# A decode attention block with a long cache: softmax and PV moved into the loop round of their own head, loads K K V V, one score buffer

## The chip, the cores and the metric

One core of one Trainium2 chip. The metric is the device time of one execution in microseconds (us). The kernel before takes 422.17 us, the median of three runs (422.05 to 422.44). Verdicts call a difference of under 2% "same".

## The reference, cut to what matters

```python
# B=2 tokens (one per batch), 32 query heads, 4 KV heads, cache of 32768 keys, head size 128
mod = (silu(c) @ w_mod)                               # 6 shifts, scales and gates
h = layernorm(x) * (1 + ca) + sa
q = h @ wq
for each of the 8 pairs (batch b, KV head g):         # 8 query heads share one KV head
    scores = q[8 heads] @ K[b, g].T * 128 ** -0.5     # K: 32768 x 128, 8.4 MB in bf16
    p = softmax(scores)
    o = p @ V[b, g]                                   # V: 8.4 MB
x = x + ga * (o @ wo)
x = x + gb * (gelu(layernorm(layernorm(x)*(1+cb)+sb) @ w1 + b1) @ w2 + b2)
```

The caches are 134 MB of the 178 MB that have to be read. From here on a "head" is one of the eight pairs (b, g).

## The kernel before

K lies in memory with keys as rows, and the score matmul needs it turned. So for each head TensorE (PE) transposes 256 tiles of 128 keys, eight to a PSUM bank; VectorE (DVE) and ScalarE (ACT) copy the banks to SBUF; and PE multiplies each turned tile with the eight queries. ACT copies the scores to SBUF, DVE takes the maxima, ACT does eight exps (one for each query head), and PE multiplies with V.

The kernel is written as a software pipeline. PE and DVE run a hardware loop with one round per head. Round i transposes K of head i and computes its scores; the "lagged" parts do softmax and PV of head i-1 in between. The last head's softmax and PV stand after the loop. All loads go in one list, in order, through the queue of SyncE (SP). K and V move in halves of 4 MB; the ring has one slot for each: first K half, second K half, first V half, second V half.

```python
def tr(i, cc, g8):   # eight transposes into psKT[g8 % 4], then one eviction by DVE or ACT
    ...
def qk(i, cc, g8):   # eight score matmuls; after each chunk cc: ACT copies scores, DVE takes the max
    ...
        Sc = S_sb[i % 2][:, :, cc * TPC:(cc + 1) * TPC]      # two score buffers
    ...
# order of loads
add_kv("K", 0, 0); add_kv("K", 0, 1)
order = [("K", 0), ("V", 0), ("K", 1), ("V", 1)]
early = [("V", 0), ("K", 0), ("K", 1), ("V", 1)]
for i in range(1, NBG + 1):
    for kind, hf in early if i == 1 else order:
        if kind == "V":  add_kv("V", i - 1, hf)
        elif i < NBG:    add_kv("K", i, hf)
# the loop, one round per head
for i in range(NBG):
    lagged(softmax_1)                            # lagged: of head i - 1, skipped in the first round
    for cc in range(NCH):                        # 4 chunks of 8 groups of 8 tiles
        for g8 in range(TPC // 8):
            tr(i, cc, g8)
            pipe.append((i, cc, g8))
            if len(pipe) > PIPE: qk(*pipe.pop(0))
            if (cc, g8) == (0, 1):   lagged(softmax_2)
            elif (cc, g8) == (0, 4): lagged(softmax_3)
            elif i and (0, 4) < (cc, g8) and exps: exp(i - 1, exps.pop(0))
        if cc == 1:   lagged(lambda: pv(i - 1, 0), row_sums, lambda: pv(i - 1, 1))
        elif cc == 3: lagged(lambda: pv(i - 1, 2), lambda: pv(i - 1, 3))
    lagged(extract)
    while pipe: qk(*pipe.pop(0))
    lagged(lambda: extract_2(i - 1))
...
# after the loop: softmax, PV and extraction of the last head, then wo, w1, w2
```

## Time and profile before

| what | value |
|---|---|
| time, median | 422.17 us |
| share of the 16 DMA engines' span in use by the load queue | 98.9% |
| bytes | 178.3 MB, 434 GB/s between first load (3.9 us) and last landing (414.5 us) |
| PE waiting for K | 45.1 us |
| period of a head | 38.7 us |

The page of the profile follows in lines. The first line is PE's busy time. The next four are 40 equal slices of the span: PE's busy tenths, the granted PE clock in tenths, the DMA engines' busy tenths, and GB/s. Then come the load queue, the shares of the chain that ended last, and two groups of instructions (the transposes of K and the PV matmuls) with busy time, mean ns of one, and idle time before them.

```profile
...
PE 296.6 (71%) x5171; PEld 237.6 (57%) x5171; DVE 166.9 (40%) x347; ACT 156.2 (37%) x269; POOL 6.0 (1%) x31
...
PE   1547429869988767695969686976859693645566
...
PEclk9999999988999997988888896989887888655575
DMA  8999999999999999999999999999999999999995
GB/s 335 430 430 420 437 440 443 411 437 446 409 443 443 424 430 443 433 421 443 440 418 443 437 418 440 443 415 440 449 412 440 446 416 437 423 429 423 428 426 244
...
q1 hardware_dynamic: 9714, 178.28, 98.9%
...
DMA 70%; PE 26%; ACT 2%; SPq 1%; issue 0%; DVE 0%
...
L543 PE MATMUL psKT<-ident,K 128*128 128x128 bf16 x2048 | 174.0, 237 | 46.1 <-DMA K<-in_A_k_cache_dram 45.1
...
L586 PE MATMUL psO<-V,E_sb 128*32 128x512 bf16 x512 | 33.9, 401 | 1.3 <-ACT E_sb L576 1.3
...
```

DMA is at nine tenths in every slice between the first and the last. That is the sign of a kernel bound by its loads: no engine's work can shorten it, as long as no wait holds the loads up. The Trainium skill ("DMA: Bandwidth & Descriptors", Bandwidth, Where 436 GB/s comes from) gives 435 GB/s as the ceiling of the ports into SBUF; this trace shows 434.

The view of waits (who waited for whom, us in total, times, longest) says how PE stands to the loads:

```profile
...
PE psKT L543 <- DMA K<-in_A_k_cache_dram: 45.1, 13, 6.4
...
```

PE waits 13 times for K, which is slack of PE. Here is PE in one round, from the timeline (start, us, engine, line, operation, output<-inputs, count, and in brackets the idle time before it and what ended it):

```profile
...
295.45 0.62 PE L543 MATMUL psKT<-ident,K 128*128 128x128 bf16 x8 [3.72 <-DMA K<-in_A_k_cache_dram]
...
307.18 1.91 PE L586 MATMUL psO<-V,E_sb 128*32 128x512 bf16 x32
309.02 0.76 PE L555 MATMUL psS<-qcur,KT_sb 128*128 128x8 bf16 x24
310.79 0.48 PE L606 MATMUL psM<-msum,hmat 128*128 128x128 f32 x2 [1.01 <-DVE msum L601]
314.75 1.89 PE L543 MATMUL psKT<-ident,K 128*128 128x128 bf16 x16 [3.48 <-DMA K<-in_A_k_cache_dram]
...
```

PE starts the second half of K when it lands (295.45), does PV of the head before at 307.18 in the middle of the stream, and then waits 3.48 us for the next head's K. After the loop the last head's softmax and PV ran alone, with nothing under them:

```profile
...
348.94 0.75 PE L555 MATMUL psS<-qcur,KT_sb 128*128 128x8 bf16 x24
...
349.73 0.60 ACT L559 ACTIVATE S_sb<-psS 128x512 f32<-128x512 f32 x1 [2.33 <-PE psS L555]
...
353.93 0.51 ACT L576 ACTIVATE E_sb<-S_sb,negm 128x256 bf16<-128x256 f32 x1 [3.60 <-DVE negm L572]
...
358.99 0.23 DVE L593 COPY rsum<-rowsum 128x128 f32<-128x128 f32 x1 [5.16 <-ACT E_sb L576]
...
359.79 5.83 PE L586 MATMUL psO<-V,E_sb 128*32 128x512 bf16 x64
...
```

From the end of the last scores (349.7) to the first exp 4.2 us (0.8 of which is another head's work on DVE), eight exps to 359.0, and 64 PV matmuls in 5.83 us. The other PV groups of before take 1.05 to 1.9 us for 16 to 32 matmuls.

### The profile page before, as it was taken

How to read it: one execution, taken by the hardware profiler on the slowest of the kernel's cores; microseconds unless marked ns; L12 is line 12 of the kernel's file. 1: busy time of each engine (PE TensorE's matmuls, PEld its weight loads, DVE VectorE, ACT ScalarE, POOL GpSimd, SP SyncE). 2: the span in 40 equal slices, each digit the busy share in tenths (PEclk: the TensorE clock that was granted, in tenths of full speed). 3: DMA queues.
4: the chain of work that ended last, by engine and by line, in shares of the span. 5: the costliest groups of instructions: out<-in, count | busy, mean ns of one | idle time of the engine just before them, and what ended most of it. 6: DMA issues, size and time to landing. Idle time of an engine off the chain costs nothing.

```text
span 420.3 us, 11591 instructions
## 1 busy us (share of the span) xinstructions
PE 296.6 (71%) x5171; PEld 237.6 (57%) x5171; DVE 166.9 (40%) x347; ACT 156.2 (37%) x269; POOL 6.0 (1%) x31
## 2 busy tenths in 40 slices
PE   1547429869988767695969686976859693645566
PEld 1105109859878657494949575764849492212244
DVE  1102005645676454354536452653555363101311
ACT  2000005538548334551636282446426364200020
POOL 3000000000000000000000000000000000000000
PEclk9999999988999997988888896989887888655575
DMA  8999999999999999999999999999999999999995
GB/s 335 430 430 420 437 440 443 411 437 446 409 443 443 424 430 443 433 421 443 440 418 443 437 418 440 443 415 440 449 412 440 446 416 437 423 429 423 428 426 244
DMA packets 9727, 178.46 MB, mean 425 GB/s; under 512 B 1002, under 2 KB 1009, under 8 KB 2291
## 3 DMA queue, kind: packets, MB, share of 16 engines
q1 hardware_dynamic: 9714, 178.28, 98.9%
q8 instruction: 9, 0.15, 0.1%
q14 instruction: 4, 0.02, 0.0%
HBM read 178.28 MB, written 0.00 MB: 424 GB/s over the span
## 4 chain that ended last, share of the span: by engine, by line
DMA 70%; PE 26%; ACT 2%; SPq 1%; issue 0%; DVE 0%
DMA K<-in_A_k_cache_dram 51%; PE psKT L543 18%; DMA wo<-in_A_wo_dram 8%; DMA w<-in_B_w_dram 7%; PE psS L555 5%; DMA wmod<-in_w_mod_dram 4%; ACT E_sb L576 1%; PE psO L586 1%; SPq L415 1%; ACT KT_sb L547 1%; PE psO L759 1%; PE psS L680 0%; ACT L576 0%; PE psM L566 0%; ACT S_sb L559 0%
## 5 line engine op out<-in xcount | busy, mean ns | idle before, releaser
L543 PE MATMUL psKT<-ident,K 128*128 128x128 bf16 x2048 | 174.0, 237 | 46.1 <-DMA K<-in_A_k_cache_dram 45.1
L543 PEld LDWEIGHTS psKT<-ident,K 128*128 128x128 bf16 x2048 | 133.7, 106 | 53.7 <-DMA K<-in_A_k_cache_dram 49.2
L549 DVE COPY KT_sb<-psKT 128x1024 bf16<-128x1024 bf16 x160 | 107.8, 689 | 107.0 <-PE psKT L543 107.0
L547 ACT ACTIVATE KT_sb<-psKT 128x1024 bf16<-128x1024 bf16 x96 | 98.0, 1021 | 128.4 <-PE psKT L543 128.4
L555 PE MATMUL psS<-qcur,KT_sb 128*128 128x8 bf16 x2048 | 88.1, 167 | 7.7 <-ACT KT_sb L547 6.4
L555 PEld LDWEIGHTS psS<-qcur,KT_sb 128*128 128x128 bf16 x2048 | 79.0, 98 | 12.7 <-ACT KT_sb L547 7.6
L576 ACT ACTIVATE E_sb<-S_sb,negm 128x256 bf16<-128x256 f32 x64 | 32.3, 504 | 8.1 <-DVE negm L572 7.1
L586 PE MATMUL psO<-V,E_sb 128*32 128x512 bf16 x512 | 33.9, 401 | 1.3 <-ACT E_sb L576 1.3
L560 DVE TENSOR_REDUCE m1c<-psS 128x8 f32<-128x512 f32 x32 | 22.1, 690 | 14.8 <-ACT S_sb L559 14.1
L559 ACT ACTIVATE S_sb<-psS 128x512 f32<-128x512 f32 x32 | 18.9, 592 | 18.9 <-PE psS L555 18.9
L586 PEld LDWEIGHTS psO<-V,E_sb 128*32 128x32 bf16 x512 | 12.2, 100 | 13.1 <-issue 4.2
L491 PE MATMUL psS<-wmod,inT 128*32 128x512 bf16 x64 | 8.4, 622 | 11.9 <-DMA wmod<-in_w_mod_dram 11.9
L680 PE MATMUL psS<-wo,atT 128*32 128x512 bf16 x64 | 7.6, 627 | 10.8 <-DMA wo<-in_A_wo_dram 10.8
L462 ACT ACTIVATE stat<-stat 128x2 f32<-128x2 f32 x3 | 0.6, 203 | 35.4 <-DVE stat L461 35.4
L512 PE MATMUL psS<-wq,inT 128*32 128x512 bf16 x64 | 7.6, 627 | 7.1 <-DMA wq<-in_A_wq_dram 6.1
L576 ACT ACTIVATION_READ_ACCUMULATOR E_sb<-S_sb,negm 128x1 f32 x64 | 12.1, 189 | 0.0
L491 PEld LDWEIGHTS psS<-wmod,inT 128*32 128x32 bf16 x64 | 1.3, 112 | 17.9 <-DMA wmod<-in_w_mod_dram 17.4
L680 PEld LDWEIGHTS psS<-wo,atT 128*32 128x32 bf16 x64 | 1.9, 128 | 15.4 <-DMA wo<-in_A_wo_dram 9.4
L606 PE MATMUL psM<-msum,hmat 128*128 128x128 f32 x16 | 4.2, 346 | 7.1 <-DVE msum L601 7.1
L497 ACT ACTIVATE S_sb<-psS 128x512 f32<-128x512 f32 x1 | 0.6, 597 | 22.8 <-DVE S_sb L499 22.8
L499 DVE COPY S_sb<-psS 128x512 f32<-128x512 f32 x1 | 0.7, 692 | 20.6 <-PE psS L491 20.6
L599 DVE TENSOR_SCALAR msum<-psO,mk 128x128 f32<-128x128 f32 x8 | 2.8, 351 | 15.0 <-PE psO L586 15.0
(116 smaller groups left out, 136.4 us busy)
## 6 DMA issues: line engine op xcount, KB each, us to landing
K<-in_A_k_cache_dram SPq DMA_DIRECT2D x16, 4096.0 KB, 25.6
V<-in_A_v_cache_dram SPq DMA_DIRECT2D x16, 4096.0 KB, 32.5
wmod<-in_w_mod_dram SPq DMA_DIRECT2D x8, 1536.0 KB, 16.4
wq<-in_A_wq_dram SPq DMA_DIRECT2D x4, 2048.0 KB, 37.7
wo<-in_A_wo_dram SPq DMA_DIRECT2D x4, 2048.0 KB, 25.3
w<-in_B_w_dram SPq DMA_DIRECT2D x4, 1792.0 KB, 35.8
w<-in_B_w_dram SPq DMA_DIRECT2D x3, 2048.0 KB, 30.4
w<-in_B_w_dram SPq DMA_DIRECT2D x1, 768.0 KB, 27.9
```

Source lines behind the costliest of these rows:

```text
L415: T.dma("sp", lambda e, dst=dst, src=cur.src: e.dma_start(dst, src), key=cur.sem, writes=[cur.reg], frees=old)
L491: pe(lambda e, w=it.view, k=k, ch=ch, n=n, q=q: e.matmul(bank[n][32 * q:32 * q + 32, :], lhsT=inT[:, k, :], rhs=w[:, ch * 512:(ch + 1) * 512],
L512: pe(lambda e, w=it.view, k=k, ch=ch, n=n, q=q: e.matmul(bank[n][32 * q:32 * q + 32, :], lhsT=inT[:, k, :], rhs=w[:, k % 2, ch * 512:(ch + ...
L543: pe(lambda e, kq=kq, jj=jj, w=kt, t=t: e.transpose(psKT[kq][:, jj * 128:(jj + 1) * 128], w[:, t, :], ident[:, :]), reads=[it.reg, "ident" ...
L547: act(lambda e, src=src: e.activation(KT_sb[g8][:, :, :], src, ACT.Copy), reads=[f"psKT{kq}"], writes=[f"KT_sb{g8}"], sem=f"ev{cc}_{g8}")
L549: dve(lambda e, src=src: e.tensor_copy(KT_sb[g8][:, :, :], src), reads=[f"psKT{kq}"], writes=[f"KT_sb{g8}"], sem=f"ev{cc}_{g8}")
L555: pe(lambda e, t=t, jj=jj: e.matmul(ps[:, t * HPG:(t + 1) * HPG], lhsT=KT_sb[g8][:, jj, :], rhs=qcur[:, :], start=True, stop=True), reads= ...
L559: act(lambda e: e.activation(Sc, ps[:, :].rearrange("p (t h) -> p h t", h=HPG), ACT.Copy), reads=[preg], writes=[f"S_sb{i % 2}_{cc}"], sem ...
L560: dve(lambda e: e.tensor_reduce(m1c[:, :, cc], ps[:, :].rearrange("p (t h) -> p h t", h=HPG), AX.X, ALU.max), reads=[preg], writes=[f"m1c{ ...
L576: act(lambda e: e.activation(E_sb[:, :, h, :], S_sb[j][:, h, :].rearrange("p (u t) -> p u t", t=4), ACT.Exp, bias=negm[:, h:h + 1], scale= ...
L586: pe(lambda e, t4=t4, tg=tg, q=q: e.matmul(psO[32 * q:32 * q + 32, :], lhsT=E_sb[:, tg // 4, :, :].rearrange("p h t -> p (h t)"), rhs=vt[: ...
L680: pe(lambda e, w=it.view, g=g, j=j, hf=hf, q=q: e.matmul(psS[0][32 * q:32 * q + 32, :], lhsT=atT[g][:, j, :], rhs=w[:, j, hf * 512:(hf + 1 ...
```

## The change

The intent is a simpler loop: each head is finished in its own round, first K, then V, with no "lagged" parts, no branches in the loop, one score buffer in place of two, and no attention code after the loop. The price is that PE stands still while the softmax of a head runs. The work itself (bytes, matmuls, copies, exps) is unchanged.

```diff
-    S_sb = [sb(f"S_sb{i}", [128, HPG, NT]) for i in range(2)]
+    S_sb = sb("S_sb", [128, HPG, NT])
...
-    add_kv("K", 0, 0)
-    add_kv("K", 0, 1)
-    order = [("K", 0), ("V", 0), ("K", 1), ("V", 1)]
-    early = [("V", 0), ("K", 0), ("K", 1), ("V", 1)]
-    for i in range(1, NBG + 1):
-        for kind, hf in early if i == 1 else order:
-            if kind == "V":
-                add_kv("V", i - 1, hf)
-            elif i < NBG:
-                add_kv("K", i, hf)
+    for i in range(NBG):
+        for kind in "KV":
+            for hf in range(2):
+                add_kv(kind, i, hf)
...
     for i in range(NBG):
-        lagged(softmax_1)
         for cc in range(NCH):
             for g8 in range(TPC // 8):
                 tr(i, cc, g8)
...
-                if (cc, g8) == (0, 1):
-                    lagged(softmax_2)
-                elif (cc, g8) == (0, 4):
-                    lagged(softmax_3)
-                elif i and (0, 4) < (cc, g8) and exps:
-                    exp(i - 1, exps.pop(0))
-            if cc == 1:
-                lagged(lambda: pv(i - 1, 0), row_sums, lambda: pv(i - 1, 1))
-            elif cc == 3:
-                lagged(lambda: pv(i - 1, 2), lambda: pv(i - 1, 3))
-        lagged(extract)
         while pipe:
             qk(*pipe.pop(0))
-        lagged(lambda: extract_2(i - 1))
+        softmax_1()
+        softmax_2()
+        softmax_3()
+        for h in range(HPG):
+            exp(h)
+        row_sums()
+        for cc in range(NCH):
+            pv(i, cc)
+        extract()
+        extract_2(i)
...   (cut: the helper that folds the rounds into a loop loses its lagged parts; the copy of
       softmax, PV and extraction after the loop goes; ring offsets of the K and V halves and of w1 move)
```

More of the change, by code (lines that the diff above doesn't have):

```diff
@@ L34 @@
 RING = 160 * 1024
+AHEAD = ("sc2", "sc3", "pk", "ac")
 EVAC_PATTERN = ("dve", "act", "dve", "act", "dve", "dve", "act", "dve")
@@ L41 @@
     LOOPED = ("pe", "dve")
-    PE_KEYS = ("pe", "pl")
     def __init__(self, nc):
@@ L55, in __init__ @@
         self.segments = None
-        self.lag = False
     def key(self, name, given=0, step=None):
@@ L116, in _dep_tokens @@
         if E == "pe":
-            tokens = [t for t in tokens if t[0] not in self.PE_KEYS]
+            tokens = [t for t in tokens if t[0] != "pe"]
         return tokens
@@ L130, in _put @@
         if self.segments is not None and E in self.LOOPED:
-            self.segments[E][-1][1].append(op)
+            self.segments[E].append(op)
         else:
@@ L168, in raw @@
         self._put(E, ("raw", [], fn, None))
-    def part(self, lag):
-        self.lag = lag
-        for E in self.LOOPED:
-            self.segments[E].append((lag, []))
     def fold(self, rounds):
@@ L180, in _fold @@
         first = min(rounds)
-        full = rounds[max(rounds)]
         body = []
-        for n, (lag, ops) in enumerate(full):
-            merged = []
-            for k, (kind, _, fn, extra) in enumerate(ops):
-                offs = {}
-                for it, segs in rounds.items():
-                    same, other = segs[n]
-                    assert same == lag
-                    if not other and lag and it == first:
-                        continue
-                    assert len(other) == len(ops) and other[k][0] == kind and other[k][3] == extra
-                    for key, val in other[k][1]:
-                        off = val - self.step[key] * it
-                        assert offs.setdefault(key, off) == off, (E, n, k, key, it, val, offs)
-                waits = []
-                for key, off in offs.items():
-                    assert self.step[key] * (first + lag) + off > 0, (E, n, k, key, off)
-                    waits.append((key, self.step[key], off))
-                merged.append((kind, waits, fn, extra))
-            if merged:
-                body.append((lag, merged))
+        for k, (kind, _, fn, extra) in enumerate(rounds[max(rounds)]):
+            offs = {}
+            for it, ops in rounds.items():
+                assert len(ops) == len(rounds[first]) and ops[k][0] == kind and ops[k][3] == extra
+                for key, val in ops[k][1]:
+                    off = val - self.step[key] * it
+                    assert offs.setdefault(key, off) == off, (E, k, key, it, val, offs)
+            for key, off in offs.items():
+                assert self.step[key] * first + off > 0, (E, k, key, off)
+            body.append((kind, [(key, self.step[key], off) for key, off in offs.items()], fn, extra))
         self.ops[E].append(("loop", [], body, (first, max(rounds) + 1)))
@@ L218, in _loop @@
     def _loop(self, eng, E, body, bounds):
-        pairs = [w[1:] for _, ops in body for op in ops for w in op[1]]
+        pairs = [w[1:] for op in body for w in op[1]]
         often = [p for p in dict.fromkeys(pairs) if p != (1, 0) and pairs.count(p) > 1]
@@ L227, in wait @@
                 eng.wait_ge(self.sem[w[0]], val[w[1:]] if w[1:] in val else it * w[1] + w[2])
-            for lag, ops in body:
-                def run():
-                    for op in ops:
-                        self._emit(eng, E, op, wait)
-                if lag:
-                    with eng.If(it > bounds[0]):
-                        run()
-                else:
-                    run()
+            for op in body:
+                self._emit(eng, E, op, wait)
     def emit(self, block):
@@ L272, in bass_adaLN_cond__gqa_block_cached__mixer_channel_mlp__decode_kernel @@
     T = Tracker(nc)
-    for name, step, given in (("pe", 64, 0), ("pl", 8, 8), ("dve", 4, 0), ("dl", 4, 4)):
-        T.key(name, given)
-        T.step[name] = step
+    T.step["pe"], T.step["dve"] = 72, 8
     def sb(name, shape, dtype=FP32):
@@ L331, in bass_adaLN_cond__gqa_block_cached__mixer_channel_mlp__decode_kernel @@
     rinv = sb("rinv", [128, 1])
-    S_sb = [sb(f"S_sb{i}", [128, HPG, NT]) for i in range(2)]
-    row = S_sb[0].rearrange("p h n -> p (h n)")
-    ROW = [f"S_sb0_{cc}" for cc in range(NCH)]
+    S_sb = sb("S_sb", [128, HPG, NT])
+    row = S_sb.rearrange("p h n -> p (h n)")
+    ROW = [f"S_sb_{cc}" for cc in range(NCH)]
     E_sb = sb("E_sb", [128, NT // 4, HPG, 4], BF16)
@@ L368, in add @@
         by_key[key] = it
-    SLOT = {("K", 0): 0, ("V", 0): 1, ("K", 1): 2, ("V", 1): 3}
     def add_kv(kind, i, hf):
@@ L376, in add_kv @@
         add((kind, i, hf), [2, TPC * D], cache[b, g][r0:r0 + 2 * CH_ROWS, :].rearrange("(p c t) d -> p c (t d)", c=2, p=128),
-            SLOT[kind, hf] * 32 * KB, f"{kind}{hf}")
+            ((64 if kind == "V" else 0) + hf * 32) * KB, f"{kind}{hf}")
     wm_v = w_mod.rearrange("(p k) n -> p k n", k=KT8)
@@ L383, in bass_adaLN_cond__gqa_block_cached__mixer_channel_mlp__decode_kernel @@
         add(("wq", k), [2, HQ * D], A_wq[k * 256:(k + 1) * 256, :].rearrange("(k p) n -> p k n", p=128), (96 + 16 * k) * KB)
-    add_kv("K", 0, 0)
-    add_kv("K", 0, 1)
-    order = [("K", 0), ("V", 0), ("K", 1), ("V", 1)]
-    early = [("V", 0), ("K", 0), ("K", 1), ("V", 1)]
-    for i in range(1, NBG + 1):
-        for kind, hf in early if i == 1 else order:
-            if kind == "V":
-                add_kv("V", i - 1, hf)
-            elif i < NBG:
-                add_kv("K", i, hf)
+    for i in range(NBG):
+        for kind in "KV":
+            for hf in range(2):
+                add_kv(kind, i, hf)
     for g, off in enumerate((128, 144, 0, 16)):
         add(("wo", g), [8, DM], A_wo[g * 1024:(g + 1) * 1024, :].rearrange("(p j) n -> p j n", j=8), off * KB)
-    for k, off in enumerate((64, 80, 32, 48)):
+    for k, off in enumerate((32, 48, 64, 80)):
         add(("w1", k), [2, F], B_w1[k * 256:(k + 1) * 256, :].rearrange("(k p) n -> p k n", p=128), off * KB)
@@ L420, in dve @@
     def dve(fn, reads=(), writes=(), sem=None):
-        T.inst("dve", fn, reads=reads, writes=writes, sem=sem or ("dl" if T.lag else None))
+        T.inst("dve", fn, reads=reads, writes=writes, sem=sem)
     def act(fn, reads=(), writes=(), sem=None):
@@ L426, in pe @@
     def pe(fn, reads=(), writes=(), mark=True):
-        T.inst("pe", fn, reads=reads, writes=writes, mark=mark, sem="pl" if T.lag else None)
+        T.inst("pe", fn, reads=reads, writes=writes, mark=mark)
     need("wmod", 0)
@@ L522, in bass_adaLN_cond__gqa_block_cached__mixer_channel_mlp__decode_kernel @@
     dve(lambda e: e.tensor_copy(qT[:, :, :], psM[:, 0:64].rearrange("p (b h) -> p b h", b=2)), reads=["psM"], writes=["qT"], sem="mo")
-    for name in ("sc2", "sc3", "pk", "ac"):
-        T.key(name, 1)
-        T.raw("pe", lambda e, name=name: e.sem_inc(T.sem[name], 1))
-    for name in ("pl", "dl"):
-        T.raw("pe", lambda e, name=name: e.sem_inc(T.sem[name], T.step[name]))
+    for name in AHEAD:
+        T.key(name, T.step.get(name, 1))
+        T.raw("pe", lambda e, name=name: e.sem_inc(T.sem[name], T.step.get(name, 1)))
     T.wait("pe", reads=["ident", "identf", "onesf", "hmat"], writes=["psS0", "psS1", "psO", "psM"] + [f"psKT{q}" for q in range(NPKT)])
@@ L557, in qk @@
         if g8 == TPC // 8 - 1:
-            Sc = S_sb[i % 2][:, :, cc * TPC:(cc + 1) * TPC]
-            act(lambda e: e.activation(Sc, ps[:, :].rearrange("p (t h) -> p h t", h=HPG), ACT.Copy), reads=[preg], writes=[f"S_sb{i % 2}_{cc}"], sem=f"sc{cc}")
+            Sc = S_sb[:, :, cc * TPC:(cc + 1) * TPC]
+            act(lambda e: e.activation(Sc, ps[:, :].rearrange("p (t h) -> p h t", h=HPG), ACT.Copy), reads=[preg], writes=[f"S_sb_{cc}"], sem=f"sc{cc}")
             dve(lambda e: e.tensor_reduce(m1c[:, :, cc], ps[:, :].rearrange("p (t h) -> p h t", h=HPG), AX.X, ALU.max), reads=[preg], writes=[f"m1c{cc}"])
@@ L572, in softmax_3, with exp @@
         dve(lambda e: e.tensor_scalar(negm[:, :], psM[:, 128:128 + HPG], -SCALE, None, ALU.mult), reads=["psM"], writes=["negm"], sem="nm")
-    def exp(i, h):
-        j = i % 2
-        act(lambda e: e.activation(E_sb[:, :, h, :], S_sb[j][:, h, :].rearrange("p (u t) -> p u t", t=4), ACT.Exp, bias=negm[:, h:h + 1], scale=SCALE,
+    def exp(h):
+        act(lambda e: e.activation(E_sb[:, :, h, :], S_sb[:, h, :].rearrange("p (u t) -> p u t", t=4), ACT.Exp, bias=negm[:, h:h + 1], scale=SCALE,
                                    accum_out=rowsum[:, h:h + 1]),
-            reads=[f"S_sb{j}_{cc}" for cc in range(NCH)] + ["negm"], writes=["E_sb", "rowsum"], sem="ex" if h == HPG - 1 else None)
+            reads=ROW + ["negm"], writes=["E_sb", "rowsum"], sem="ex" if h == HPG - 1 else None)
     def pv(i, cc):
@@ L620, in bass_adaLN_cond__gqa_block_cached__mixer_channel_mlp__decode_kernel @@
         T.segments = rounds[i + 1] = {E: [] for E in T.LOOPED}
-        def lagged(*fns):
-            T.part(True)
-            if i:
-                for fn in fns:
-                    fn()
-            T.part(False)
-        T.part(False)
-        exps = list(range(HPG))
-        lagged(softmax_1)
         for cc in range(NCH):
@@ L639, in bass_adaLN_cond__gqa_block_cached__mixer_channel_mlp__decode_kernel @@
                     qk(*pipe.pop(0))
-                if (cc, g8) == (0, 1):
-                    lagged(softmax_2)
-                elif (cc, g8) == (0, 4):
-                    lagged(softmax_3)
-                elif i and (0, 4) < (cc, g8) and exps:
-                    exp(i - 1, exps.pop(0))
-            if cc == 1:
-                lagged(lambda: pv(i - 1, 0), row_sums, lambda: pv(i - 1, 1))
-            elif cc == 3:
-                lagged(lambda: pv(i - 1, 2), lambda: pv(i - 1, 3))
-        lagged(extract)
         while pipe:
             qk(*pipe.pop(0))
-        lagged(lambda: extract_2(i - 1))
+        softmax_1()
[8 more added lines that the diff above has]
+        extract_2(i)
         T.segments = None
     T.fold(rounds)
-    T.lag = True
     for r0, r1 in ((0, 1), (1, 3), (3, 7), (7, 8)):
@@ L660, in bass_adaLN_cond__gqa_block_cached__mixer_channel_mlp__decode_kernel @@
     T.dma("sp", lambda e: e.dma_start(b1m[:, :], B_b1.rearrange("(q r) -> q r", r=512)), key="ld_b1", writes=["b1m"])
-    last = NBG - 1
-    softmax_1()
-    softmax_2()
-    softmax_3()
-    for h in range(HPG):
-        exp(last, h)
-    row_sums()
-    for cc in range(NCH):
-        pv(last, cc)
-    extract()
     for g in range(G):
         it = need("wo", g)
-        if g == 1:
-            extract_2(last)
         for j in range(8):
```

## The prediction

> **What bounds it now.** The DMA queue. The page gives 98.9% of the 16 engines' time to it, and the chain of waits is 70% DMA. 178.3 MB move between the first load (3.9 us) and the last landing (414.5 us): 434 GB/s, which is the 435 GB/s fabric ceiling that the Trainium skill ("DMA: Bandwidth & Descriptors", Bandwidth) states. A head's K and V (16.8 MB) take 38.7 us: second K halves start at 140.6, 179.3, 218.0, 256.7, 295.4, 334.2 in the timeline. PE waits 45 us for K.
>
> **What the change does.** Bytes, matmuls, evictions and exps stay. It removes the overlap: softmax, exp and PV of head i ran under the transposes of head i+1; now PE stands still for them, then does PV, extraction, and only then the next head. Loads come K,K,V,V instead of K,V,K,V; one buffer instead of two costs nothing, because the same ACT writes and reads it in order.
>
> **Cost of one serial head on PE**, from the timeline (the old tail after the loop already runs this chain serially):
> - 32 groups of eight transposes and eight score matmuls, 0.645 us each at full clock (1.07 at half clock), plus drain: 21.1
> - last score to first exp (S copy 0.60, max 0.68, small chain 1.93): 3.5
> - eight exps with accumulator reads: 5.05
> - row sums to first PV: 0.8
> - PV, 64 matmuls: 5.8 in the tail. PE is cold after the pause; the Trainium skill ("TensorE: Matmul & The Clock Gate", Part 1) says an idle window of about 3.4 us halves the clock. The trace agrees: 0.107 us each until 364.4 us, then half. I take 5.9
> - extraction: 1.5 DVE, 0.5 PE, gaps: 2.15
>
> Sum 38.5 us; I take 38.7 with occasional cold K starts. That equals the DMA period of 38.7. So PE goes from having slack to just keeping up.
>
> **How much is critical.** Head 0 starts at 63.0 as now (K lands then), about 4.4 us late from cold start and the first-round stalls seen there. Estimate: 63.0 + 4.4 + 8 x 38.7 = attention done at 377. The last wo slice lands at 382.8; the earlier wo slices need under 6 us. From there about 36 us of chain to the end, as now. PE may therefore reach about 380.5 before anything shows: about 3 us of slack over eight heads. Each us per head above 39.1 costs 8 us. The queue itself shouldn't starve: a slot is needed again 13 to 17 us after its expected release, so a lag below 10 us leaves DMA full. Nothing makes it faster: bytes and rate stay.
>
> **Prediction:** 422.6 us, 80% range 421.0 to 428.0. Faster by over 2%: 0.01; within 2%: 0.91; slower by over 2%: 0.08.
>
> **What would show it.** Right: DMA stays at 8 to 9 tenths in all slices, about 425 GB/s; PE has one pause of about 9 us per head between the last scores and PV, released by exp; PE's wait for K falls from 45 us to under 20; head period 38.7; last load lands near 414.5; granted clock low in PV, high in most of K. ACT's and DVE's busy time unchanged.
> Wrong: head periods of 40 us or more with no wait for K; wo matmuls starting after 381 without waiting for DMA; queue gaps.
>
> **What would make it wrong.** A half-clock start of every K phase (+1.4 to 2.7 us a head, from 1.07 against 0.645 a group): PE then bounds, total up to 430 to 437. Or a loop-branch cost on PE that the old loop hid (at 123.5 us K follows the last matmul with no gap, so I expect none). Or lag above 13 us, when V slots come free late and the queue runs dry.

## The result, and the profile after

The changed kernel takes 422.09 us (422.01 to 422.22, 4 runs) against 422.12 us for the kernel before (422.05 to 422.44, 4 runs). The ratio is 0.9998, with a 95% interval of 0.9981 to 1.0015: the same. Ratios are the mean time of one kernel's fast runs over that of the other's of the same rounds, so not quite the ratio of the medians quoted.

The page after, with the same lines and one group more (the row-sum matmul that ends the softmax pause):

```profile
...
PE 285.4 (68%) x5171; PEld 224.3 (53%) x5171; DVE 167.2 (40%) x347; ACT 159.4 (38%) x269; POOL 6.0 (1%) x31
...
PE   1547429846992897589379848965892798445666
...
PEclk9999999986996899699689958995997799595575
DMA  8999999999999999999999999999999999999995
GB/s 339 429 430 424 444 427 448 421 425 443 427 424 444 437 418 443 437 424 440 443 418 437 443 421 437 443 418 434 446 421 430 446 433 418 428 430 422 428 426 237
...
q1 hardware_dynamic: 9714, 178.28, 98.9%
...
PE 50%; DMA 30%; ACT 11%; DVE 6%; issue 2%; SPq 1%; ACTq 0%
...
L507 PE MATMUL psKT<-ident,K 128*128 128x128 bf16 x2048 | 153.8, 220 | 7.7 <-DMA K<-in_A_k_cache_dram 6.4
...
L549 PE MATMUL psO<-V,E_sb 128*32 128x512 bf16 x512 | 43.9, 518 | 0.0
...
L557 PE MATMUL psM<-onesf,rsum 128*128 128x1 f32 x16 | 4.7, 362 | 45.4 <-DVE rsum L556 45.4
...
```

Four things are to be seen. The DMA slices are as full as before, and GB/s too. PE's busy slices have a gap every three to four slices now: one pause per head. The clock row dips to between 5 and 7 at these pauses. And the last chain, which was 70% DMA, is 50% PE and 30% DMA. Transposes got shorter (237 to 220 ns: K is no longer started cold after a wait) and PV matmuls longer (401 to 518 ns).

Waits of PE, after:

```profile
...
PE psM L557 <- DVE rsum L556: 45.4, 8, 5.9
...
PE psKT L507 <- DMA K<-in_A_k_cache_dram: 6.4, 1, 6.4
...
```

PE's wait for K fell from 45.1 us to the one wait at the start, 6.4 us. In its place there are eight waits for the row sums at the end of the exps, 45.4 us in all. Most of PE's idle time changed its name. It is no longer slack, though: PE now waits inside its own chain (for the exps) and not for the loads.

One head from its last scores to the next head's first transposes, all engines (lines of other engines cut):

```profile
...
162.81 1.30 PE L519 MATMUL psS<-qcur,KT_sb 128*128 128x8 bf16 x32
...
164.15 0.60 ACT L523 ACTIVATE S_sb<-psS 128x512 f32<-128x512 f32 x1 [0.76 <-PE psS L519]
...
167.65 0.51 ACT L539 ACTIVATE E_sb<-S_sb,negm 128x256 bf16<-128x256 f32 x1 [2.90 <-DVE negm L536]
...
173.00 0.59 PE L557 MATMUL psM<-onesf,rsum 128*128 128x1 f32 x2 [5.65 <-DVE rsum L556]
173.51 5.10 PE L549 MATMUL psO<-V,E_sb 128*32 128x512 bf16 x64
...
180.24 0.49 PE L569 MATMUL psM<-msum,hmat 128*128 128x128 f32 x2 [1.62 <-DVE msum L564]
...
180.72 1.46 PE L507 MATMUL psKT<-ident,K 128*128 128x128 bf16 x23
...
```

The scores end at 164.1, the first exp starts at 167.65, the last ends about 172.7, PV runs from 173.51 to 178.6, extraction holds PE until 180.24, and K of the next head starts at 180.72 with no wait. The starts of the eight heads' transposes on PE are 62.85, 104.88, 142.91, 180.72, 218.39, 257.72, 296.15 and 334.11. The first interval is 42.0 us; the mean of the other six is 38.2 (229.23 / 6). Loads deliver a head in 38.7.

And where attention ends and the output projection starts:

```profile
...
371.83 2.04 PE L617 MATMUL psS<-wo,atT 128*32 128x512 bf16 x32
377.65 1.69 PE L617 MATMUL psS<-wo,atT 128*32 128x512 bf16 x16 [3.79 <-DMA wo<-in_A_wo_dram]
382.52 1.90 PE L617 MATMUL psS<-wo,atT 128*32 128x512 bf16 x16 [3.17 <-DMA wo<-in_A_wo_dram]
...
```

Two of the four wo matmul groups run at 371.83 at once, the other two still wait for their loads. Attention is done about 11 us before the last wo slice lands.

### The profile page after: what moved, and what is told of

Same layout as the page of the kernel before. It is cut to its first block, busy times and chain, and to the rows that moved or that the text cites. A ratio compares the mean times of both kernels' runs of the same rounds, so it can differ in the third digit from the quotient of the medians.

```text
span 420.3 us, 11460 instructions
## 1 busy us (share of the span) xinstructions
PE 285.4 (68%) x5171; PEld 224.3 (53%) x5171; DVE 167.2 (40%) x347; ACT 159.4 (38%) x269; POOL 6.0 (1%) x31
## 4 chain that ended last, share of the span: by engine, by line
PE 50%; DMA 30%; ACT 11%; DVE 6%; issue 2%; SPq 1%; ACTq 0%
PE psKT L507 27%; PE psS L519 10%; DMA K<-in_A_k_cache_dram 10%; PE psO L549 9%; DMA wo<-in_A_wo_dram 9%; ACT E_sb L539 8%; DMA w<-in_B_w_dram 7%; DMA wmod<-in_w_mod_dram 4%; DVE msum L564 2%; ACT KT_sb L511 2%; DVE m1c L524 1%; ACT S_sb L523 1%; PE psM L557 1%; PE psM L535 1%; PE psM L569 1%
## 5 line engine op out<-in xcount | busy, mean ns | idle before, releaser
L507 PE MATMUL psKT<-ident,K 128*128 128x128 bf16 x2048 | 153.8, 220 | 7.7 <-DMA K<-in_A_k_cache_dram 6.4
L507 PEld LDWEIGHTS psKT<-ident,K 128*128 128x128 bf16 x2048 | 118.1, 98 | 9.2 <-DMA K<-in_A_k_cache_dram 6.6
L519 PEld LDWEIGHTS psS<-qcur,KT_sb 128*128 128x128 bf16 x2048 | 76.8, 96 | 1.8 <-ACT KT_sb L511 1.4
L549 PE MATMUL psO<-V,E_sb 128*32 128x512 bf16 x512 | 43.9, 518 | 0.0
L557 PE MATMUL psM<-onesf,rsum 128*128 128x1 f32 x16 | 4.7, 362 | 45.4 <-DVE rsum L556 45.4
L549 PEld LDWEIGHTS psO<-V,E_sb 128*32 128x32 bf16 x512 | 16.3, 125 | 23.7 <-issue 19.1
L557 PEld LDWEIGHTS psM<-onesf,rsum 128*128 128x128 f32 x16 | 4.0, 310 | 46.2 <-DVE rsum L556 46.2
L556 DVE COPY rsum<-rowsum 128x128 f32<-128x128 f32 x8 | 1.8, 227 | 41.5 <-ACT E_sb L539 41.5
L530 PE MATMUL psM<-identf,m 128*8 128x128 f32 x16 | 3.2, 281 | 13.1 <-DVE m L527 13.1
L569 PEld LDWEIGHTS psM<-msum,hmat 128*128 128x128 f32 x16 | 2.4, 188 | 16.9 <-DVE msum L564 16.9
```

Source lines behind the costliest of these rows:

```text
L507: pe(lambda e, kq=kq, jj=jj, w=kt, t=t: e.transpose(psKT[kq][:, jj * 128:(jj + 1) * 128], w[:, t, :], ident[:, :]), reads=[it.reg, "ident" ...
L519: pe(lambda e, t=t, jj=jj: e.matmul(ps[:, t * HPG:(t + 1) * HPG], lhsT=KT_sb[g8][:, jj, :], rhs=qcur[:, :], start=True, stop=True), reads= ...
L549: pe(lambda e, t4=t4, tg=tg, q=q: e.matmul(psO[32 * q:32 * q + 32, :], lhsT=E_sb[:, tg // 4, :, :].rearrange("p h t -> p (h t)"), rhs=vt[: ...
L557: pe(lambda e: e.matmul(psM[:, 144:145], lhsT=rsum16.rearrange("p h e -> p (h e)"), rhs=onesf[:, 0:1], start=True, stop=True), reads=["one ...
L569: pe(lambda e: e.matmul(psM[:, 256:384], lhsT=hmat.rearrange("p h e -> p (h e)"), rhs=msum[:, :], start=True, stop=True), reads=["hmat", " ...
```

## The experiments

The theory: DMA bounds both kernels; the change lengthened PE's chain until it is as long as the loads, with a slack of some microseconds at the end that hides it. Rivals: PE bounds the changed kernel as much as DMA does (no slack); or the loads run so far ahead that PE's delays are simply absorbed; or the overlap was worth nothing in PE time. Twelve runs were made, in three batches: eleven altered kernels and the changed kernel again. All passed the comparison with the reference, even the three with less V, which are wrong. The likely reason is that V's share in the result is too small for the tolerance to see it; so this comparison hardly tests the attention itself.

### 1. More serial work: two, four or eight exps of each head done twice

```diff
+        for h in range(2):             # 4, 8 in the other runs
+            exp(h % (HPG - 1))         # the same exp again: same result, 0.63 us
         for h in range(HPG):
             exp(h)
```

Two:

> The changed kernel with two of the eight exps of each head done twice (same result): 0.63 us each, so the serial PE chain grows by about 1.27 us a head, 10 us in all. Theory (DMA bounds, PE has about 9 us of slack up to the wo matmuls): about 423.3 us, 422 to 425. Rival 1 (PE and DMA both bound, no slack): 432. Rival 2 (the loads run ahead, PE delay is absorbed): 422.1.

Four:

> Four exps of each head done twice: +2.53 us a head, 20 us in all. Theory: slack used up, about 11 us slower, 433 us (430 to 436), PE never waiting for K after head 0. Rival 1 (no slack): 442. Rival 2 (absorbed): 422.1.

Eight:

> All eight exps of each head done twice: +5.06 us a head, 40.5 us in all. Theory: 40.5 less 9 of slack, about 453.5 us (449 to 457), the DMA queue with holes late in the loop since V slots come free too late. Rival 1: 462.6. Rival 2: 422.1.

| exps doubled | time, us (lowest to highest) | ratio (95%) | span of the profiled run | wo matmuls start on PE |
|---|---|---|---|---|
| 0 (the changed kernel) | 422.09 (422.01 to 422.22) | 0.9998 (0.998 to 1.002) | 420.3 | 371.83 |
| 2 | 426.22 (423.23 to 427.84) | 1.007 (1.001 to 1.013) | 424.6 | 385.94 |
| 4 | 433.61 (432.79 to 435.25) | 1.027 (1.023 to 1.031) | 431.1 | 394.12 |
| 8 | 454.38 (453.51 to 455.83) | 1.076 (1.072 to 1.080) | 451.7 | 414.97 |

Four and eight came out as the theory had it, and both rivals are out: 442 and 462.6 without slack, 422.1 with absorption. From four to eight doubled exps the start of wo moves by 20.9 us and the span by 20.6, so there PE bounds fully. In the runs with 2, 4 and 8 the span ends 38.7, 37.0 and 36.7 us after the start of wo. So a span of 420.3 allows wo to start as late as 381.6 to 383.6, and the changed kernel (371.83) had 10 to 12 us of slack in its profiled run.

Two was a miss: 426.2 for an expected 423.3. The end of attention in that run:

```profile
...
377.96 5.94 PE L549 MATMUL psO<-V,E_sb 128*32 128x512 bf16 x64
...
385.94 3.64 PE L619 MATMUL psS<-wo,atT 128*32 128x512 bf16 x64
...
```

Here the wo matmuls run all 64 in a row, without a wait. Attention ended 14.1 us later than in the changed kernel, for about 10 us of added exps. The rest is luck of the clock: this PV took 5.94 us (5.07 us in the last head of the changed kernel), the first head's 6.52, and PV of all eight heads 46.3 us in place of 43.9; K of the first head took 2.1 us longer. With the exps these parts come to 14.6 us, so nothing is left over. The four runs spread over 4.6 us, those of the changed kernel over 0.2.

### 2. The same eight exps doubled in the kernel before

```diff
-    def exp(i, h):
+    def exp(i, h, again=True):
+        if again:
+            exp(i, h, False)
...   (cut: only the second of the two signals the end of the exps)
```

> The kernel before with the same eight exps of each head done twice. There they run under the next head's transposes: theory 422 us, within 0.5%; only the last head's serial tail grows by 5 us and its wo slack takes that. If ScalarE's extra work slowed the evictions enough, 430 or more.

Measured: 424.99 us (424.80 to 425.26), ratio 1.0055 (1.002 to 1.009). The same 40 us of ScalarE work that cost the changed kernel 32 us cost this one under 3 us. That is what the overlap had bought. The remaining 2.6 us were not foreseen. GB/s by the microsecond from 95 to 135 us, from the DMA view of the kernel before and then of this run:

```profile
...
GB/s 459 524 492 492 393 229 492 492 524 459 393 262 492 492 533 393 328 393 492 492 492 426 229 459 524 459 492 393 262 492 492 492 459 426 262 492 492 492 459 295
...
```

```profile
...
GB/s 459 492 524 524 328 262 459 524 524 459 295 360 459 532 229 0 459 66 524 524 492 229 360 492 524 524 426 197 426 524 524 524 295 262 492 524 524 524 262 295
...
```

The queue of this run was empty at 110 us (0 GB/s) and nearly so at 112 (66 GB/s). In the second round the slower evictions delayed the last transposes of K's first half, and the load waiting for that slot was issued at 110.44 us in place of 106.40. From 95 to 135 us 16.43 MB were moved in place of 17.41; the 0.98 MB missing are an estimated 2.3 us at 434 GB/s, most of the 2.7 us by which the span is longer. So the kernel before has little room early in the loop; the changed kernel has no such hole there.

### 3. Less V: the bound of DMA taken away from both

V halves of heads 1 to 7 load only 0.25 of their 4 MB (the result is wrong). Loads then need about 20 us a head.

```diff
+            src = cur.src
+            if cur.key[0] == "V" and cur.key[1] > 0:
+                dst, src = cur.view[:, 0:1, 0:1024], cur.src[:, 0:1, 0:1024]
...   (cut: the load then takes this src)
```

The changed kernel:

> The changed kernel loading each V half of heads 1 to 7 only in a small part (0.25 of 4 MB; wrong result on purpose), so that DMA no longer bounds. Theory: PE's own serial chain then shows: 62.9 + 42 + 7 x 38 + wo 3.6 + 35 of tail = about 410 us span, 408 to 416 us timed, only 3% faster, no waits for K. Rival (PE had lots of hidden slack): DMA alone would need under 300 us, so below 380.

The kernel before:

> The kernel before with the same cut in V loads (wrong result on purpose). Theory: its overlapped PE chain is about 28.5 us a head: about 346 us (335 to 362). If overlap were worth nothing it would be near 410 like the changed kernel.

The changed kernel: 412.20 us (410.26 to 412.92), ratio 0.974 (0.970 to 0.977). Taking 55 MB, 31% of all bytes, away won 10 us. Heads 1 to 7 start on PE every 38.2 us ((336.29 - 106.97) / 6), the very period that the changed kernel has with all its loads:

```profile
...
106.97 1.96 PE L510 MATMUL psKT<-ident,K 128*128 128x128 bf16 x32
...
336.29 1.96 PE L510 MATMUL psKT<-ident,K 128*128 128x128 bf16 x32
...
```

So PE was already running without a break there, and loads were not what set its pace.

The kernel before: 365.80 us (361.38 to 367.07; two of the five runs counted as slow and left out of the ratio), ratio 0.867 (0.864 to 0.870). Its head period, over the five intervals between these extraction matmuls, is 29.2 us, near the 28.5 that was expected:

```profile
...
122.87 0.48 PE L609 MATMUL psM<-msum,hmat 128*128 128x128 f32 x2 [1.01 <-DVE msum L604]
...
269.05 0.48 PE L609 MATMUL psM<-msum,hmat 128*128 128x128 f32 x2 [1.01 <-DVE msum L604]
...
```

So the overlap is worth 9.0 us of PE time a head, and the rival by which it was worth nothing is out. The time was a miss: it was expected at 346 (335 to 362) and came out 20 us higher; the profiled run, 361.38, was the fastest of the five. The list of loads goes out in order, and V of the last head waits for its slots: the weights after it were issued only at 298.40 us, and their 23.1 MB, an estimated 53 us at 434 GB/s, cannot end before 352. DMA bounds the end again, by a late start.

### 4. The clock: PE kept busy in the pause

Needless transposes of the identity, 24, 8 and 78 of them, in the three waits of the softmax pause; once with less V, once with all loads.

```diff
         softmax_1()
+        keep_warm(24)      # transposes of ident into a free PSUM bank
         softmax_2()
+        keep_warm(8)
         softmax_3()
+        keep_warm(78)
...   (cut: the helper keep_warm)
```

With less V:

> The changed kernel with less V and with 110 needless transposes in the softmax pause of each head, so that TensorE does not go to half clock. Theory: PV falls from about 5.3 to 3.5 us, 13 to 16 us less in all than the run with less V alone: about 397 us. Rival (the clock is not what makes PV slow): equal or slower.

With all loads:

> The changed kernel with all loads and the same needless transposes. Theory: DMA bounds, so 422.1 us within 0.3%, with PE now waiting for K about 1.5 us in most heads. Rival (PE bounds the changed kernel as much as DMA does): about 10 us faster.

With less V: 394.28 us (392.12 to 395.75), 18 us less than the run with less V alone (ratios to before 0.933 and 0.974). PV of one head in the run with less V, from the timeline, and then in this run:

```profile
...
175.77 5.29 PE L552 MATMUL psO<-V,E_sb 128*32 128x512 bf16 x64
...
```

```profile
...
169.71 3.64 PE L552 MATMUL psO<-V,E_sb 128*32 128x512 bf16 x64
...
```

All eight heads have 3.64 us, against 5.0 to 6.5 in the changed kernel: half the clock was what made PV slow. The head period fell from 38.2 to 36.0 us. The gain was a little over the 13 to 16 us expected.

With all loads: 422.21 us (422.18 to 422.26), ratio 0.9987 (0.996 to 1.002). PE became 2 us a head faster and the time did not move; PE now waits for K again in five of the heads (0.49 to 2.79 us), besides the 6.4 us before the first:

```profile
...
PE psKT L507 <- DMA K<-in_A_k_cache_dram: 14.8, 6, 6.4
...
```

The rival by which PE bounds the changed kernel as much as DMA does, with 10 us to be won, is out: the loads are the floor, the slack is what PE has left.

### 5. The order of loads

The changed kernel with the old order of a head's four loads.

```diff
-        for kind in "KV":
-            for hf in range(2):
+        for hf in range(2):
+            for kind in "KV":
                 add_kv(kind, i, hf)
```

> The changed kernel with the loads of a head in the order of before (first K half, first V half, second K half, second V half). The second K half then lands 19.4 us after the first in place of 9.7, while PE needs it 10.6 us after its start, so each head starts up to 9 us behind its first landing. Theory: attention ends near 380, at the edge of the slack: 422 to 424.5 us. If the order were worth nothing: 422.1; if PE had no slack: 430.

Measured: 489.92 us (487.47 to 490.98), ratio 1.157 (1.153 to 1.160). Every one of the three expectations was far off. The DMA slices of its page:

```profile
...
DMA  8999999919993999399929992999299939999995
GB/s 349 425 428 429 431 445 442 433 66 403 443 435 122 403 430 432 126 392 438 446 99 430 430 430 97 438 438 441 92 430 430 430 129 430 430 421 424 426 428 239
...
```

Once per head the queue runs nearly dry (66 to 129 GB/s in a slice). Its loads on SP, from the timeline:

```profile
...
109.28 0.33 SPq L381 DMA_DIRECT2D V<-in_A_v_cache_dram  x1
109.65 0.43 SPq L381 DMA_DIRECT2D K<-in_A_k_cache_dram  x1
111.00 0.33 SPq L381 DMA_DIRECT2D V<-in_A_v_cache_dram  x1
122.81 0.33 SPq L381 DMA_DIRECT2D K<-in_A_k_cache_dram  x1
...
```

The first V half of head 1 can go out only when PV of head 0 has freed its slot, at 109.28 us. The second K half of head 1 stands behind it in the list and goes out at 109.65, although its own slot had been free since head 0's K was transposed. But head 1 cannot reach its PV without that K half. Waits for K:

```profile
...
PE psKT L507 <- DMA K<-in_A_k_cache_dram: 66.6, 9, 8.2
...
```

66.6 us in nine waits, 6.4 of which the changed kernel has too; the 60.2 us more are most of the 67.7 us of longer span. The Trainium skill ("DMA: Bandwidth & Descriptors", Anatomy of one DMA) says that "any semaphore wait happens on the issuing sequencer before dispatch". Its section describes loads issued by GpSimd; these go out on SP, and the trace agrees: SP's queue waits 261.4 us for PV and 127.1 us for score matmuls. This run shows what follows from it: a load whose slot is not free holds up all loads after it. In a kernel that finishes a head before it starts the next, and has one slot for each half, all of K has to stand before V in the list. The order of loads is not a detail of this change but what makes it possible.

### 6. The single score buffer

The changed kernel with two score buffers again.

```diff
-    S_sb = sb("S_sb", [128, HPG, NT])
+    S_sb = [sb(f"S_sb{i}", [128, HPG, NT]) for i in range(2)]
...
-            Sc = S_sb[:, :, cc * TPC:(cc + 1) * TPC]
+            Sc = S_sb[i % 2][:, :, cc * TPC:(cc + 1) * TPC]
...   (cut: the exps read the buffer of their head)
```

> The changed kernel with two score buffers again, as before the change. Theory: ScalarE fills and empties the buffer in its own order, so nothing waits on it: 422.1 us, and the same pauses of PE. If the single buffer cost something, PE's pause before PV would shrink.

Measured: 422.28 us (422.14 to 422.51), ratio 0.9981 (0.995 to 1.001); the changed kernel itself had 422.28 in the same batch. PE's wait for the row sums is 45.4 us, as in the changed kernel. The second buffer is worth nothing here.

### 7. The changed kernel again, and its slack restored

> The changed kernel again, in five rounds, since the kernel before had runs up to 424.5 us in the earlier batches. Theory: in the profiled run PE's chain ended 9.8 us ahead of where it would show (371.9 against about 381.7), and the clock's luck in PV is worth at most 1.6 us a head, so every run at 422.0 to 422.6. If the PE chain already mattered, runs of 424 and more as in the run with two exps doubled.

Measured: 422.28 us (422.05 to 422.68, 6 runs), ratio 0.9981 (0.996 to 1.001). In the profiled run wo starts at 375.11, 3.3 us later than in the first profile, and the span is 420.4 against 420.3: PE's chain moves by microseconds between runs and the time does not follow. Of the 3.3 us, 2.8 arise in the first head, 44.8 us in place of 42.0: PE stands still there for 1.67 us in place of 0.85, for no cause that the profile shows, and from 84 to 88 us the granted clock is 0.62 and then 0.53 in place of 1.00. The kernel before scattered more in the same rounds, 422.04 to 424.83.

The run with two exps doubled, with the needless transposes of experiment 4 (98 in place of the last 78):

> The run with two exps of each head doubled (426.2 us, 423.2 to 427.8) with 130 needless transposes in the softmax pause. Theory: full clock in PV takes back 1.5 to 3 us a head, PE's chain falls inside its slack again: 422.2 us, and all runs within 0.3 us. Rival (the scatter of that run was of another origin): still 423 to 428.

Measured: 423.43 us (423.38 to 423.49), ratio 1.0008 (0.998 to 1.004). The spread fell from 4.6 to 0.1 us, and PE waits for K again in two heads, so the chain is within its slack again. That fits a scatter of PE's clock but does not single it out: any shorter chain would hide its scatter, and the run with less V kept warm (experiment 4) still spread over 3.6 us. But the time is 1.2 us above the expected 422.2. In the profile all of it lies in the last load, whose matmuls start at 415.86 us in place of 414.55 in the run with all loads and a warm clock, while the last wo slice comes only 0.2 us later. The cause of that last microsecond was not found.

## Why the prediction was right

It forecast 422.6 us (421.0 to 428.0); 422.09 was measured. Point by point:

- **DMA bounds before and after: right.** DMA slices and GB/s are the same in both profiles, and taking 2 us a head from PE (experiment 4, all loads) changes nothing.
- **The price of a serial head: right, by the parts.** Head 2, forecast and measured in us: K phase 21.1 and 21.2, last scores to first exp 3.5 and 3.5, exps 5.05 and 5.1, row sums 0.8 and 0.8, PV 5.9 and 5.1, extraction 2.15 and 2.1. The sum was 38.5 (taken as 38.7); the mean period is 38.2. All these terms were read from the profile of before, all but the K phase from its serial tail. The largest error is PV, whose half-clock part varies: 5.0 to 6.5 us.
- **PE from slack to just keeping up: right.** The wait for K fell from 45.1 us to 6.4, all of it before the first head.
- **Half clock in PV, full clock in K: right.** Experiment 4 shows that the clock, not the matmuls, made PV 5.0 to 6.5 us: 3.64 when kept busy. The half-clock start of every K phase, feared in the prediction, did not come: in heads 1 to 7 the first transposes take 61 ns each (32 in 1.96 us).
- **The slack: right in kind, too small in size.** The prediction had attention end at 377 with 380.5 allowed, about 3 us. Measured are 371.8 in the first profile and 375.1 in the second, with 381.6 to 383.6 allowed by experiment 1: about 10 to 12 us and 6.5 to 8.5. Mis-sized were the head period, 0.5 us too long in six intervals, the last head, 1.0 us too long, and the first head: 43.1 us forecast, 42.0 and 44.8 measured in the two profiles. That the first head fell near its forecast is in part luck, since it depends on a dip of the clock (experiment 7).
- **The one buffer costs nothing: right** (experiment 6).
- **The order of loads: passed over.** The prediction named it as a mere rearrangement and only checked that slots come free in time. With the old order the same serial loop takes 490 us (experiment 5).
- **What the tie hides.** The overlap is worth 9.0 us of PE time a head (experiment 3, 38.2 against 29.2). It was off the critical path, since loads set 38.7. The change spent nearly all of it: 40 us of extra serial work cost the changed kernel 32 us and the kernel before under 3.

One thing stays open. The kernel before had 11 runs of 29 above 422.7 us (up to 424.83) over all batches; the ten of the changed kernel stayed at or below 422.68. The hole in its queue that experiment 2 provoked early in the loop is a candidate, but no trace of one of those slower runs was taken.

## What to carry to other kernels

From this one kernel: when loads bound, overlap between compute stages can be given up for free until the serial chain of a round is as long as the loads of that round. Work out that sum from a place where the stages already run alone, such as the tail after a pipelined loop, and then ask how much slack is left, because the kernel has become sensitive to everything that was hidden. And when the order of the work changes, the order of the loads in an in-order queue has to change with it: ask of each load which work must be done before its slot is free, and whether that work needs a load standing behind it.

## What the Trainium skill lacked or had wrong

- "TensorE: Matmul & The Clock Gate", Part 4 (PE-mode transpose), says that the full clock does not engage for transposes because they do not count as PE activity in the same way. Here 110 transposes in the softmax pause kept PE at full clock (78 in 4.53 us, and PV at 3.64 us after them, against 5.0 to 6.5 us after a pause without them), and the granted clock of the run was 0.946 against 0.859. That transposes alone bring a cold PE to full clock is not shown. The kernel issues them as the language's transposes into a bf16 PSUM bank; whether the page means another form, no run here tells.
- The same page, Part 1, gives windows of about 3.4 us for the clock and calls the ramp under 1% of a typical span. That is said of one ramp at a kernel's start and is not wrong for it; pauses that repeat, which the page treats under HAM oscillation, cost more. Here a pause of 9 us per head with two small matmuls in it costs 1.4 to 2.9 us of PV in every head: the 18 us that experiment 4 won are 4% of its time.
- "DMA: Bandwidth & Descriptors" (Anatomy of one DMA) says that waits for semaphores stand on the issuing sequencer, but not what follows for a ring of slots behind one queue: a load that waits for its slot holds up all loads after it. Here that cost most of 67.7 us of span (experiment 5) and a late start of the weights (experiment 3).
- The same page, Bandwidth: its table has 425 GB/s for a single core at 16 MB, but the text on where 436 GB/s comes from says that for transfers from HBM the HBM side, about 358 GB/s, is the limit. Here one core held 434 GB/s from HBM for 410 us, close to the ceiling of 435 for the ports; so that sentence is too low for a core that loads alone, which its own table shows too.
